# Gated mix of linear attention and a state-space convolution: from four groups of token rows with carries to one group of sixteen rows

## The chip, the core and the metric

The kernel runs on one core of one Trainium2 chip. The metric is the device time of one execution in microseconds (us). The core has five engines, each with its own in-order queue: PE (matrix products), DVE (vector), ACT (scalar functions), POOL (GpSimd) and SP (issues transfers). They wait for each other through semaphores. A transfer that adds to what stands at its destination is issued from POOL here; plain loads and stores are issued from SP.

## What is computed

With x of 2048 tokens by 448 channels, cut to what matters:

```python
x = A_x
g = sigmoid((x * gate_w).sum(-1, keepdims=True))
q, k, v = x @ wqkv                         # 16 heads of 28 channels
pq, pk = phi(q), phi(k)                    # phi(t) = t + 1 if t > 0 else exp(t), + 1e-6
a = (pq @ (pk^T v)) / (pq @ sum(pk)) @ wo  # head by head, no causal mask
K = 2 * Re(sum_n C[d, n] * exp(A[d, n] * dt[d] * l))
b = causal_convolution(x, K) + x * D_skip
out = g * a + (1 - g) * b
```

For the parameters at hand the taps K of a channel do not change over the 2048 lags at the accuracy kept. The kernel tests this per channel (flags in `okc`), and a channel that passes has as convolution its running sum over the tokens times one number (`near`, the same for every token). Where a channel fails, `general_conv` computes all of it after the main part; in these runs it isn't entered.

## The kernel before

The tokens are cut into 16 chunks of 128, a chunk being one row of each of the 128 partitions. Products are made with operands split into a high and a low part, so each projection of a chunk is 11 matmuls. The program is written in the order in which each engine executes it (a manual schedule): a call like `split_t(c)` puts one instruction on ACT and one on POOL at that place in their queues.

**Stage one** (lines 466 to 585, chunks 0 to 13 in the loop with index `c`): per iteration PE makes the k projection of chunk c+1, the q projection of chunk c, and the sums `g` over tokens (x against phi(k), 11 matmuls, `do_g`). ACT and DVE turn projections into phi (`k_feature`, `k_high`, `k_low`, `q_post`); POOL makes the low parts (`low`) and x * D_skip into `y` (`skip`). The bank `k` in PSUM is written by each k projection, so `k_low` of one chunk on DVE stands ahead of the next k projection on PE.

**The running sum of the tokens** goes along with stage one. Chunks form 4 groups of 4 (G = 4). Within a group, partition p holds four consecutive tokens, one in each chunk. So a group's running sum consists of: two adding transfers along the four rows of a partition (`running_a`, `running_b`); a strictly lower triangular product over the partitions of the rows' totals on PE (`group_split`, `group_heads`, two matmuls with `tri`); per pair of chunks, the addition of these heads and the product with `near` on DVE (`convolve`); and an adding transfer of the result into `y` (`group_add`). What the earlier groups add to all tokens of a later group is not added to `y`: a group's last row goes by a small transfer into `u`, a matmul (`inter`, line 749) sums the rows of the earlier groups, and the result enters the output product of each chunk as extra contraction rows, against rows of the gate 1 - g, which two transposes on PE (`gates_b`), ACT, DVE and 15 small transfers (`phi`) prepare and which ACT copies into each chunk's operand (`tail`).

**The join** (lines 696 to 841): the last two chunks; the sum of phi(k) over all tokens (`zo`, then `zb` on ACT); POOL multiplies phi(q) with it (`norm_a`, L595); DVE reduces that to the denominators (`norm_b`, L600) and inverts them (`norm_d`); POOL and DVE scale phi(q) (`norm_c`). PE makes `kv_products` (L780, `k` and `tr`), DVE masks and splits them (`kv_split`, `kv_low`), ACT makes `kvh`, and PE multiplies with the output weights (`m_products`, L760, tiles `m`). Parts of the result go through four transfers of SP (`wk<-shl`, L820 and L821) to the partitions where stage two wants them.

**Stage two** (lines 866 to 894): per chunk 4 transposes (`tr`, L657), 11 matmuls (`a`, L683), the final sum a + (1 - g) * y on DVE (`final_b`) and the store.

Names that the steps below use: `wo` is the output weight, `woh`/`wol` its split parts (ACT copy and POOL subtraction, L584 and L243); `homes` are the buffers of the running sums; `gate` (L406 to L408) turns the gate sums of 14 chunks into 1 - g on DVE.

Of the kernel before, what the change touches and what calls it, by code (L numbers as in the profile page):

```python
# [15 lines left out]
P = 128  # L16
# [18 lines left out]
G = 4  # L35
SMALL = 2.0 ** -70
# [4 lines left out]
RX = DT + 3 * NC  # L41
# [3 lines left out]
UL = 32  # L45
UZ = 4 * UL
# [7 lines left out]
def general_conv(ctx: ExitStack, tc: tile.TileContext, ga, y, og, okc, both, gin_d, out):  # L54
# [80 lines left out]
    grouped = lambda t: t.rearrange("(g p r) d -> p g (r d)", p=P, r=G)  # L135
    ygr = yg.rearrange("p (g r) d -> p g (r d)", r=G)
    SP.dma_start(out=ygr, in_=grouped(nat))
# [4 lines left out]
    SP.dma_start(out=grouped(out), in_=ygr)  # L142
# [3 lines left out]
def gated_mix_kernel(ctx: ExitStack, tc: tile.TileContext, xin, wq_d, wvo_d, abc_d, ldt_d, dsk_d,  # L146
# [21 lines left out]
    wvo = const.tile([P, 2, J, D], F32, name="wvo")  # L168
    wv, wo = wvo[:, 0], wvo[:DJ, 1]
    ident, trir = both[:, 0], both[:, 1]  # L170
    cst = const.tile([P, DJ + RX + 1], F32, name="cst")
    mask, gcat, sel = cst[:DJ, :DJ], cst[:UZ, DJ:DJ + RX], cst[:, DJ + RX:]
    gcr = const.tile([UZ, RX], F32R, name="gcr")
    ones = const.tile([P, P], F32R, name="ones")
    rows = const.tile([P, S], F32, name="rows")
    dsk = rows[:, D:2 * D]
    near, side = [], []
    u = const.tile([UZ, D], F32, name="u")
# [8 lines left out]
    spare = const.tile([P, G, D], F32, name="spare")  # L187
    room = const.tile([P, 2 * NAT + 3 * D], F32, name="room")
# [10 lines left out]
    POOL.memset(rows[DT:RX, 2 * D:], 0.0)  # L199
    POOL.memset(u, 0.0)  # L200
# [12 lines left out]
    abc = [t[:DJ, o:o + 2 * J * N].rearrange("p (i j n) -> p i j n", i=2, j=J) for t, o in ((pf, 3 * J * N), (room, 0))]  # L213
# [210 lines left out]

    homes = (wvo[:, 1], pq[:, NC - G:], room[:, :G * D].rearrange("p (r d) -> p r d", r=G), spare)
    sums, heads = {}, {}

    def group_load(g):
        SP.dma_start(out=homes[g], in_=xin[g * G:(g + 1) * G, :, NAT:LO].rearrange("r p d -> p r d"))

    def running_a(g):
        w = homes[g]
        POOL.dma_start(out=w[:, 1::2], in_=w[:, 0::2], accum_op=ALU.add)

    def running_b(g):
        w = homes[g]
        POOL.dma_start(out=w[:, 2:], in_=w[:, 1:2].to_broadcast([P, 2, D]), accum_op=ALU.add)

    def group_split(g):
        w = sums[g] = tp.tile([P, 2, D], F32R, name="sums", tag="v0", bufs=1)  # L440
        ACT.copy(w[:, 0], homes[g][:, G - 1])
        low(POOL, w[:, 1], homes[g][:, G - 1], w[:, 0])

    def group_heads(g):
        o = heads[g] = ps.tile([P, 512], F32, name="v", tag="v0")[:, :D]
        w = sums.pop(g)
        for i in range(2):
            PE.matmul(o, lhsT=tri, rhs=w[:, i], start=i == 0, stop=i == 1)  # L448

    def convolve(c):  # L450
        g, i = c // G, c % G
        a, full = homes[g][:, i:i + 2], [P, 2, D]
        DVE.tensor_tensor(out=a, in0=a, in1=heads[g][:, None, :].to_broadcast(full), op=ALU.add)
# [4 lines left out]
    def group_add(g):  # L458
        POOL.dma_start(out=y[:, g * G:(g + 1) * G], in_=homes[g], accum_op=ALU.add)
# [52 lines left out]
    group_load(0)  # L512
    for c in range(2, NC - 2):
        if c + 3 < NC:
            load_x(c + 3)
        if c == 2:
            SP.dma_start(out=cst, in_=cst_d)
        if c in (5, 6):
            group_load(c - 3)
        if c == 10:  # L520
            SP.dma_start(out=wo, in_=wvo_d[:DJ, 1])
        if c == 11:
            SP.dma_start(out=wv, in_=wvo_d[:, 0])
        ko = project(c + 1, wkh, wkl, D, "v1" if c in (2, 4) else "k")
        if c == 6:
            group_heads(0)
        if c > 6:
            convolve(2 * c - 12)
        split_t(c + 2)
        if c == 6:  # L530
            running_b(1)
        if c in (6, 8):
            running_a(c // 2 - 1)
        if c > 5:
            split_n(c + 2, False)
        k_feature(c + 1, ko)
        if c in (7, 9, 11):
            group_split(c // 2 - 2)
        if c in (7, 9):
            running_b(c // 2 - 1)  # L540
        if c > 5:
            skip(c + 2)
        k_high(c + 1)
        k_low(c + 1)
        if c == 6:
            convolve(0)
        qo = project(c, wqh, wql, D + 2, "q")
        q_post(c, qo)
        if c < 5:
            steps(2 if c == 4 else 1)  # L550
        if c == 4:
            ACT.copy(tri, trir)
            ACT.copy(gcr, gcat)
# [9 lines left out]
        if c in (7, 9, 11):  # L563
            group_heads(c // 2 - 2)
        if c < 4:
            skip(c - 1)
            skip(c + 2)
            (running_a, running_b)[c - 2](0)
        if c < 6:
            split_n(c + 2, c > 3)  # L570
        if c == 3:
            group_load(1)
        if c == 4:
            running_a(1)
        if c == 5:
            group_split(0)
        if c in (7, 9, 11, 13):
            group_add(c // 2 - 3)
        for j in {12: (0, 1), 13: (2, 3)}.get(c, ()):
            w = xn_p.tile([P, NX], F32R, name="wo", tag="n") if j < 2 else xp.tile([P, XC], F32R, name="wo", tag="xr")  # L580
            w = w[:DJ, :2 * D].rearrange("p (i d) -> p i d", i=2)
            woh.append(w[:, 0])
            wol.append(w[:, 1])
            ACT.copy(woh[j], wo[:, j])  # L584
            low(POOL, wol[j], wo[:, j], woh[j])
# [4 lines left out]
    rc = []  # L590
    pn, th, tl, pd, dn, dp = {}, {}, {}, {}, {}, []

    def norm_a(c):
        pd[c] = room[:, 2 * NAT + c % 3 * D:][:, :D]
        POOL.tensor_tensor(out=pd[c], in0=pq[:, c], in1=zb, op=ALU.mult)  # L595
# [19 lines left out]
    def norm_c(c):  # L615
        n = pn[c] = room[:, c % 2 * NAT:][:, :NAT].rearrange("p (j t) -> p j t", j=J)
# [12 lines left out]

    def phi(c):  # L630
        if 0 < c < NC:
            a = c - 1 if c < NC - 1 else 0
            i = DT + 3 * c
            SP.dma_start(out=rows[i:i + 3, c * P:(c + 1) * P], in_=phs[c // (NC - 1)][a:a + 1].bitcast(F32))

    phs = []

    def gates_a(a, b):
        return og[:, a:b]

    def gates_b(g, o):
        PE.transpose(o[:g.shape[1], :P], g, ident)

    def gates_c(n, o, tag):
        w = tp.tile([P, D], F32R, name="phs", tag=tag)[:n, :3 * P].rearrange("p (i t) -> p i t", i=3)
        phs.append(w)
        ACT.copy(w[:, 0:2], o[:n, None, :P].to_broadcast([n, 2, P]))
        return lambda: DVE.tensor_tensor(out=w[:, 2], in0=o[:n, :P], in1=w[:, 0].bitcast(F32), op=ALU.subtract)
# [18 lines left out]
    def tail(c):  # L667
        ACT.copy(tl[c][DT:RX, 3], rows[DT:RX, c * P:(c + 1) * P])

    av = {}  # L670
    oview = out.rearrange("(g p r) d -> g r p d", p=P, r=G)

    def attend(c, cuts):
        av[c] = []
        h, l = th.pop(c), tl.pop(c)
        for i, (lo, hi) in enumerate(cuts):
# [4 lines left out]
            seq += [(h[:, 3], mh[:, 3]), (l[:RX, 3], rc[0][:RX])]  # L681
# [36 lines left out]
    norm_a(0)  # L718
    norm_a(1)
    gate(c, c + 1)  # L720
    POOL.memset(rows[DT:RX, :D], 0.0)
    norm_bd(0)
    norm_c(0)
    norm_a(2)
    for i in range(4):
# [5 lines left out]
        if i == 2:  # L731
            gates_b(gates_a(1, NC - 1), g[0])
# [255 lines left out]
```

## Time and profile before

| | |
|---|---|
| times, 3 runs | 170.06, 170.11, 170.46 us (median 170.11) |
| the profiled execution | 170.16 us, of which the profile's span is 168.4 us |
| granted TensorE clock | 0.998 |
| DVE, ACT, POOL busy | 115.6, 107.6, 118.9 us |
| POOL's adding transfers (queue q0) | 12 issues, 7.34 MB, 23.4% of the 16 engines' time |
| transfers of SP (queue q1) | 21.81 MB, 38.4% |
| chain that ended last, by engine | PE 68%, ACT 10%, issue 3%, POOL 3%, DVE 1% |

The span begins with the first instruction and ends with the last; the 1.8 us between it and the execution's time lie around it. Times in the views count from the span's start. A row of the timeline gives the start, the duration, the engine, the line of the kernel, the operation with the tiles it writes and reads, the count, and in brackets how long the engine had been idle before it and what ended the wait. "issue" in the chain is time in which an engine waited for nothing that the profile shows.

### The profile page before, as it was taken

Reading aid. Unit: us, or ns where it says so; the run is one execution under the profiler, and the core shown is the slowest. Engines: PE = TensorE matmul, PEld = TensorE weight load, DVE = VectorE, ACT = ScalarE, POOL = GpSimd, SP = SyncE. Lnnn points to the kernel's source line nnn. Section 1 sums busy time; section 2 is a strip of 40 time slices with the busy share of each in tenths; the row PEclk is TensorE's granted clock in tenths of the full one; section 3 lists DMA queues with packets and bytes.
Section 4 is the critical chain, followed back from the end, with each engine's and each line's share of the span. In section 5 each row is a group of like instructions: output and inputs, shape, how many; then the busy total and the mean of one; then the engine's idle time right before and its main releaser. Section 6 shows DMA issues by size and latency. Waiting matters only on the chain.

```text
span 168.4 us, 2703 instructions
## 1 busy us (share of the span) xinstructions
PE 163.2 (97%) x852; PEld 146.9 (87%) x852; DVE 115.6 (69%) x230; ACT 107.6 (64%) x245; POOL 118.9 (71%) x128
## 2 busy tenths in 40 slices
PE   6899999999999999999999999999999999999992
PEld 2698999999998999999999999989879999999991
DVE  0837745685844966767568567878988989997551
ACT  3688668898395694775856687564845564574541
POOL 6082589988948999757869479749786997953100
PEclk9999999999999999999999999999999999999999
DMA  5989999999992949998999800900121221221213
GB/s 158 414 314 315 282 291 337 276 246 216 396 277 44 176 110 256 224 236 256 318 233 258 172 4 0 218 2 1 28 47 55 112 110 59 109 92 73 111 58 113
DMA packets 11750, 29.45 MB, mean 175 GB/s; under 512 B 1331, under 2 KB 8198, under 8 KB 11510
## 3 DMA queue, kind: packets, MB, share of 16 engines
q1 hardware_dynamic: 8838, 21.81, 38.4%
q0 software_dynamic: 2752, 7.34, 23.4%
q8 instruction: 7, 0.11, 0.3%
q10 hardware_dynamic: 144, 0.11, 0.2%
q14 instruction: 9, 0.07, 0.1%
HBM read 17.93 MB, written 3.67 MB: 128 GB/s over the span
## 4 chain that ended last, share of the span: by engine, by line
PE 68%; ACT 10%; issue 3%; POOL 3%; DVE 1%; ACTq 0%; POOLq 0%
PE a L683 21%; PE q L346 13%; PE g L422 13%; PE k L346 9%; PE tr L657 4%; ACT y L300 2%; PE m L760 2%; PE v L346 1%; ACT xn L253 1%; ACT y L301 1%; ACT e L374 1%; PE v L448 1%; PE k L780 1%; PE tr L780 1%; ACT xt L247 1%
## 5 line engine op out<-in xcount | busy, mean ns | idle before, releaser
L683 PE MATMUL a<-wk,th 128*128 128x448 f32 (+1 forms) x170 | 36.8, 361 | 0.1
L422 PE MATMUL g<-pkh,xn 128*128 128x448 f32 x112 | 35.8, 364 | 0.0
L683 PEld LDWEIGHTS a<-wk,th 128*128 128x128 f32 x170 | 29.5, 189 | 2.3 <-issue 0.7
L346 PE MATMUL q<-wqh,xt 128*128 128x450 f32 x120 | 27.6, 367 | 0.0
L346 PE MATMUL k<-wk,xt 128*128 128x448 f32 x121 | 26.8, 366 | 0.4 <-ACT wk L469 0.4
L243 POOL TENSOR_TENSOR xn<-xr,xn 128x448 fp32r<-128x448 f32 x16 | 22.8, 1424 | 6.1 <-ACT xn L253 6.1
L243 POOL TENSOR_TENSOR xt<-xr,xt 128x512 fp32r<-128x512 f32 x14 | 21.4, 1526 | 7.2 <-ACT xt L247 7.2
L346 PEld LDWEIGHTS k<-wk,xt 128*128 128x128 f32 x121 | 22.6, 188 | 2.8 <-ACT wk L469 0.8
L346 PEld LDWEIGHTS q<-wqh,xt 128*128 128x128 f32 x120 | 22.5, 189 | 1.7
L422 PE MATMUL g<-pkl,xn 128*128 128x448 f32 x64 | 23.4, 366 | 0.0
L259 POOL TENSOR_TENSOR y<-xr,rows 128x448 f32<-128x448 f32 x16 | 23.2, 1456 | 0.0
L422 PEld LDWEIGHTS g<-pkh,xn 128*128 128x128 f32 x112 | 21.1, 188 | 2.2
L595 POOL TENSOR_TENSOR room<-pq,zb 128x448 f32<-128x448 f32 x16 | 18.5, 1165 | 3.8 <-issue 2.7
L620 POOL TENSOR_TENSOR room<-pq,den 128x336 f32<-128x336 f32 x16 | 12.2, 763 | 7.4 <-ACT den L609 4.0
L375 DVE SCALAR_TENSOR_TENSOR k<-k,e 128x448 f32<-128x448 f32 x11 | 7.0, 632 | 12.7 <-ACT e L374 12.7
L373 ACT ACTIVATE e<-k 128x448 f32<-128x448 f32 x11 | 6.0, 545 | 13.5 <-PE k L346 13.5
L688 DVE SCALAR_TENSOR_TENSOR ot<-y,og,a 128x448 f32<-128x448 f32 (+1 forms) x17 | 10.7, 629 | 5.4 <-PE a L683 5.4
L665 DVE TENSOR_TENSOR th<-tr,th 128x512 fp32r<-128x512 f32 x16 | 11.0, 690 | 2.6 <-ACT th L664 2.0
L664 ACT CAST th<-tr 128x512 fp32r<-128x512 f32 x16 | 9.4, 588 | 5.0 <-PE tr L657 4.8
L422 PEld LDWEIGHTS g<-pkl,xn 128*128 128x128 f32 x64 | 11.2, 174 | 1.2 <-DVE pkl L385 0.2
L694 ACT COPY pq<-a 128x448 f32<-128x448 f32 (+1 forms) x17 | 8.7, 516 | 5.0 <-DVE ot L688 5.0
L346 PE MATMUL v<-wk,xt 128*128 128x448 f32 x55 | 11.8, 362 | 0.0
(183 smaller groups left out, 316.6 us busy)
## 6 DMA issues: line engine op xcount, KB each, us to landing
xr<-in SPq DMA_DIRECT2D x15, 512.0 KB, 5.9
out<-ot SPq DMA_DIRECT2D x15, 224.0 KB, 1.9
pq<-in SPq DMA_DIRECT2D x2, 896.0 KB
room<-in SPq DMA_DIRECT2D x2, 896.0 KB
wvo<-in SPq DMA_DIRECT2D x2, 896.0 KB
y<-in SPq DMA_DIRECT2D x2, 480.0 KB
y<-in SPq DMA_DIRECT2D x2, 450.0 KB
wvo<-wvo POOLq DMA_DIRECT2D x2, 448.0 KB, 5.5
```

The source lines that it names most:

```text
L243: eng.tensor_tensor(out=o, in0=r, in1=h.bitcast(F32), op=ALU.subtract)
L259: POOL.tensor_tensor(out=y[:, c], in0=plain[c][:, :D], in1=dsk, op=ALU.mult)
L346: PE.matmul(o[:, :n], lhsT=a, rhs=b, start=run.n == 1, stop=not seq)
L375: DVE.scalar_tensor_tensor(out=pks[c], in0=pks[c], scalar=1.0, in1=e, op0=ALU.add, op1=ALU.max)
L422: PE.matmul(g[i][:a.shape[1], :D], lhsT=a, rhs=b, start=c == 0 and n == 0, stop=c == NC - 1 and n == len(seq) - 1)
L595: POOL.tensor_tensor(out=pd[c], in0=pq[:, c], in1=zb, op=ALU.mult)
L620: POOL.tensor_tensor(out=n[:, :3, :DJ].rearrange("p j (h d) -> p j h d", h=4), in0=a, in1=r[:, :H - 4].rearrange("p (j h) -> p j h", j=3)[ ...
L664: ACT.copy(h, ov)
L665: DVE.tensor_tensor(out=l, in0=ov, in1=h.bitcast(F32), op=ALU.subtract)
L683: PE.matmul(a[:, lo:hi], lhsT=u_, rhs=w_[:, lo:hi], start=n == 0, stop=n == 10)
L688: DVE.scalar_tensor_tensor(out=ot[:, lo:hi], in0=y[:, c, lo:hi], scalar=og[:, c:c + 1], in1=a[:, lo:hi], op0=ALU.mult, op1=ALU.add)
L694: ACT.copy(pq[:, c, lo:hi], a[:, lo:hi])
```

## The change

The 16 chunks become one group: partition p holds the 16 consecutive tokens 16p to 16p+15, chunk c the token 16p + c. The host lays x out so, and the store writes so.

- `near` is multiplied in ahead of the sums across partitions (`slope`, one DVE product per pair of chunks; the addition of heads is gone from it).
- The running sums along a partition are still made by fours, in two buffers of 8 chunks: one `running_a` and two `running_b` per buffer. The totals of the fours are summed on POOL (`total`) into `over`.
- One split and one triangular product (`whole_split`, `whole_head`) of the totals of all 16 chunks take the place of four.
- DVE adds the head to three of the four rows of `over`, ACT copies it to the fourth (`heads`), and four adding transfers from POOL (`head_add`) add row g of `over` to the four chunks of group g in `y`.
- The carry rows, the product `inter`, the gate transposes, the 15 + 3 small transfers and the ACT copies `tail` are gone. One matmul of the last q projection (`q_run(1)`) stands where `inter` stood.
- The loads of the output and value weights come later (c = 12 and 13, in halves), since their buffer holds eight chunks of the running sum; `wo` is split at the end of c = 13 and in the part after the loop, in place of c = 12 and 13.

```diff
+SLOPES = {8: 0, 9: 4, 11: 8}
...
-    homes = (wvo[:, 1], pq[:, NC - G:], room[:, :G * D].rearrange("p (r d) -> p r d", r=G), spare)
+    homes = (wvo, room)
...
-    def convolve(c):
-        g, i = c // G, c % G
-        a, full = homes[g][:, i:i + 2], [P, 2, D]
-        DVE.tensor_tensor(out=a, in0=a, in1=heads[g][:, None, :].to_broadcast(full), op=ALU.add)
-        DVE.tensor_tensor(out=a, in0=a, in1=near[0][:, None, :].to_broadcast(full), op=ALU.mult)
-        if i and g < NC // G - 1:
-            SP.dma_start(out=u[g:UL + g + 1:UL, None], in_=homes[g][P - 1:P, G - 1:].to_broadcast([1, 2, D]))
+    def running_b(h):
+        w = homes[h].rearrange("p (g r) d -> p g r d", r=G)
+        for g in range(2):
+            POOL.dma_start(out=w[:, g, 2:], in_=w[:, g, 1:2].to_broadcast([P, 2, D]), accum_op=ALU.add)
+
+    def slope(c):
+        a = homes[c // (2 * G)][:, c % (2 * G):][:, :2]
+        DVE.tensor_tensor(out=a, in0=a, in1=near[0][:, None, :].to_broadcast([P, 2, D]), op=ALU.mult)
+
+    def total(g):
+        a = homes[g // 2][:, g % 2 * G + G - 1]
+        POOL.tensor_tensor(out=over[:, g + 1 if g < 3 else 0], in0=over[:, g] if g > 1 else homes[0][:, G - 1], in1=a,
+                           op=ALU.add)
...
+    def heads():
+        o = sums.pop()
+        ACT.copy(over[:, 0], o)
+        for g in range(1, NC // G):
+            DVE.tensor_tensor(out=over[:, g], in0=over[:, g], in1=o, op=ALU.add)
+
+    def head_add(g):
+        POOL.dma_start(out=y[:, g * G:(g + 1) * G], in_=over[:, g:g + 1].to_broadcast([P, G, D]), accum_op=ALU.add)
...
+        if c == 12:
+            slope(12)
+            slope(14)
...
+        if c in SLOPES:
+            slope(SLOPES[c])
+            slope(SLOPES[c] + 2)
...
+        if c == 13:
+            whole_head()
+            group_add(3)
+            split_o(0)
+            split_o(1)
...
     c = NC - 2
-    POOL.memset(rows[DT:RX, D:2 * D], 0.0)
+    heads()
+    for i in range(NC // G):
+        head_add(i)
     gate(0, c)
     ko = project(c + 1, wkh, wkl, D, "v1")
-    uw = xt_p.tile([P, 2 * NAT], F32R, name="uw", tag="t")[:UZ, :D]
     k_feature(c + 1, ko)
-    ACT.copy(uw, u)
-    low(POOL, uw[UL:2 * UL], u[UL:2 * UL], uw[UL:2 * UL])
+    split_o(2)
+    split_o(3)
...
-            gates_b(gates_a(1, NC - 1), g[0])
-    gates = gates_c(NC - 2, g[0], "pkl")
     norm_b(1)
-    gates()
...
-    carry = inter()
+    q_run(1)
```

The order of instructions on POOL around the end of the loop, where `xn` is the low part of the last chunk of the loop, `wo` the low parts of the output weight, and `room<-pq,zb` the first `norm_a`. Before:

```order
L243 TENSOR_TENSOR xn<-xr,xn 128x448
L259 TENSOR_TENSOR y<-xr,rows 128x448
L459 DMA y<-spare 128x1792
L243 TENSOR_TENSOR wo<-wvo,wo 112x448 x2
L697 MEMSET rows 48x448
L243 TENSOR_TENSOR uw<-u,uw 32x448
L595 TENSOR_TENSOR room<-pq,zb 128x448 x2
```

After, on the same engine at the same place (`y<-over` is `head_add`):

```order
L234 TENSOR_TENSOR xn<-xr,xn 128x448
L234 TENSOR_TENSOR sums<-over,sums 128x448
L250 TENSOR_TENSOR y<-xr,dsk 128x448
L437 DMA y<-room 128x1792
L234 TENSOR_TENSOR wo<-wvo,wo 112x448 x2
L464 DMA y<-over 128x4x448 x4
L234 TENSOR_TENSOR wo<-wvo,wo 112x448 x2
L608 TENSOR_TENSOR room<-pq,zb 128x448 x2
```

The four adding transfers, one subtraction and two of the four `wo` operations have come between the last chunk's operands and the first `norm_a`; a memset and `uw` have gone from there.

On DVE in iterations 11 and 12 (`pq<-q,e` ends `q_post`, `k<-k,e` is `k_feature`, `pkl` the last of `k_low`). Before:

```order
L400 SCALAR_TENSOR_TENSOR pq<-q,e 128x448
L453 TENSOR_TENSOR spare<-spare,v 128x896
L454 TENSOR_TENSOR spare<-spare,p 128x896
L375 SCALAR_TENSOR_TENSOR k<-k,e 128x448
L385 SCALAR_TENSOR_TENSOR zb<-k,zb 128x448
L385 SCALAR_TENSOR_TENSOR pkl<-k,pkh 128x448
```

After, between the same two iterations:

```order
L391 SCALAR_TENSOR_TENSOR pq<-q,e 128x448
L434 TENSOR_TENSOR room<-room,p 128x896 x4
L366 SCALAR_TENSOR_TENSOR k<-k,e 128x448
L376 SCALAR_TENSOR_TENSOR zb<-k,zb 128x448
L376 SCALAR_TENSOR_TENSOR pkl<-k,pkh 128x448
```

Four products stand ahead of `k_feature` where two operations of the same size stood.

More of the change, by code (lines that the diff above doesn't have):

```diff
@@ L439, in group_split, with half_load @@
[L439 to L446, printed above, removed]
+    homes = (wvo, room)
+    sums = []
+    def half_load(h, i):
+        SP.dma_start(out=homes[h][:, i * G:(i + 1) * G],
+                     in_=xin[(2 * h + i) * G:(2 * h + i + 1) * G, :, NAT:LO].rearrange("r p d -> p r d"))
@@ L628, in norm_c @@
                           in1=r[:, None, H - 4:, None].to_broadcast([P, 2, 4, DH - DS]), op=ALU.mult)
[L630 to L648, printed above, removed]
     def turn(c):
@@ L834, in gated_mix_kernel @@
     ACT.copy(mh[:DT, 3], shl[:DT, 0].bitcast(F32))
-    ACT.copy(rc[0][:DT], shl[:DT, 0].bitcast(F32))
     norm_d(2, 2, ACT.copy)
```

176 lines of the change are left out of this document (65 added, 111 removed).

## The prediction

> **What bounds the kernel now.** I read the engines' shares first, then the chain that ended last, then the timelines of PE and POOL where the change acts.
>
> ```profile
> PE 163.2 (97%) x852; PEld 146.9 (87%) x852; DVE 115.6 (69%) x230; ACT 107.6 (64%) x245; POOL 118.9 (71%) x128
> ```
>
> PE is busy nearly all the time, so only fewer PE instructions or shorter waits of PE can shorten the kernel. The chain of waits (start, length, what) says the same from 51.4 us on:
>
> ```profile
> 51.43 0.47 PE v L448
> ...
> 63.02 0.41 PE v L448 x2
> ...
> 113.46 0.11 PE g L642
> ...
> 113.97 0.21 PE z L749
> ...
> 117.44 1.34 PE m L760 x6
> ...
> 124.67 0.10 issue
> ...
> 149.36 0.11 PE o L642
> ```
>
> The reader is to see that the triangular products (v L448), the gate transposes (L642) and the carry product (z L749) are links of it, and that between z and the last chunk it stays on PE but for 0.10 us at 124.67. The rows of PE itself show the first triangular product:
>
> ```profile
> 50.94 0.96 PE L448 MATMUL v<-sums,tri 128*128 128x448 f32 x2
> 51.74 1.79 PE L346 MATMUL q<-wqh,xt 128*128 128x450 f32 x8
> ```
>
> **What the change removes on PE.** The first pair takes the slot from 50.94 to 51.74, 0.80 us, of which 0.4 are a wait; the three others 0.41 us each in the chain (63.02, and the same at 76.73 and 90.45). That is 2.02 us, and one pair of 0.41 comes back after iteration 13: -1.61. The gate transposes are 0.11 each, -0.22. Where z (0.21) stood, one of the q products now stands, which is missing later: -0.21. If all else were hidden: 168.4 - 2.04 = 166.4 us of span. Around the span lie 170.16 - 168.38 = 1.8 us, so 168.1 us; the profiled execution is within 0.05 us of the median 170.11. What must be hidden for this is next.
>
> **POOL ahead of the first norm_a.** This is the step that decides. POOL's rows around the end of stage one:
>
> ```profile
> 97.75 2.29 POOL L243 TENSOR_TENSOR wo<-wvo,wo 112x448 fp32r<-112x448 f32 x2 [3.13 <-ACT wo L584]
> 100.01 1.29 POOL L243 TENSOR_TENSOR xt<-xr,xt 128x512 fp32r<-128x512 f32 x1
> 101.27 1.15 POOL L243 TENSOR_TENSOR xn<-xr,xn 128x448 fp32r<-128x448 f32 x1
> 102.38 1.15 POOL L259 TENSOR_TENSOR y<-xr,rows 128x448 f32<-128x448 f32 x1
> 103.83 0.87 POOL L459 DMA_DIRECT2D y<-spare  x1 [0.30 <-POOL y L259]
> 104.44 2.55 POOL L243 TENSOR_TENSOR wo<-wvo,wo 112x448 fp32r<-112x448 f32 x2
> ...
> 111.94 2.26 POOL L595 TENSOR_TENSOR room<-pq,zb 128x448 f32<-128x448 f32 x2 [2.70 <-issue]
> ```
>
> Before, POOL sits idle 2.70 us ahead of 111.94: the two norm_a wait for zb, which ACT has from PE. In between now stand four head_add. What does one cost POOL? The rows of its adding transfers:
>
> ```profile
> 76.74 1.19 POOL L437 DMA_DIRECT2D spare<-spare  x1 [1.62 <-DMA spare<-spare]
> 77.52 1.61 POOL L259 TENSOR_TENSOR y<-xr,rows 128x448 f32<-128x448 f32 x1
> ...
> 65.09 2.03 POOL L433 DMA_DIRECT2D spare<-spare  x1
> 65.87 2.44 POOL L243 TENSOR_TENSOR xn<-xr,xn 128x448 fp32r<-128x448 f32 x1
> ```
>
> Behind an idle POOL, the transfer in 128 pieces of 7168 bytes (103.83) takes 0.87 us, and the one in 256 pieces of 1792 bytes (76.74) 1.19 us, although it moves half the bytes. So the pieces count: 0.32 us per 128. head_add copies one row to four, 512 pieces of 1792 bytes: **1.84 us each by that slope, 7.36 for four**. The trace has no transfer in 512 pieces. Bounds: 0.87 (only issues count) and 2.03 (the longest row, which had work queued ahead of it). I take 1.84, since 0.87 and 1.19 differ by pieces in just this direction; both ends stay in the range.
>
> Is this time on POOL's path, or does the next instruction start earlier? It starts 0.78 us after the transfer (76.74 to 77.52), but then lasts 1.61 instead of 1.15. The xn subtraction behind 65.09 lasts 2.44: the starts run ahead, the ends do not. The Trainium skill, page "Perfetto Trace Analysis", section "GPSIMD Engine Instruction", gives the opposite rule: treat a GpSimd span as unreliable and time by the start-to-start spacing. The stretched rows speak against it; what it would give here is the first rival below, 169.4 us.
>
> Now POOL's queue. In iteration 12 ACT did two wo copies ahead of the last chunk's, which are now later:
>
> ```profile
> 97.12 1.02 ACT L584 CAST wo<-wvo 112x448 fp32r<-112x448 f32 x2
> ```
>
> So that copy starts where the wo copies did, at 97.1, less 2.02 of PE, plus 0.8 from the slopes (below): 95.9, and POOL can begin at 96.5. From there without a gap: 1.29 (xt) + 1.15 (xn) + 1.15 (the sums subtraction, of xn's size) + 1.15 (y) + 0.30 + 0.87 (group_add) + 2.29 (two wo) = 8.2, so 104.7; four head_add, 112.1; two wo, 114.4; the first norm_a, **115.5**. Its natural end, by zb, is 111.94 + 1.15 = 113.1 shifted by -1.61 and the slopes' 0.3: 111.8. POOL is 3.7 us late.
>
> Who waits for it:
>
> ```profile
> 107.58 0.63 DVE L375 SCALAR_TENSOR_TENSOR v<-v,e 128x448 f32<-128x448 f32 x1
> ...
> 113.12 0.63 DVE L600 TENSOR_REDUCE den<-room 128x16 f32<-128x448 f32 x1 [0.93 <-POOL room L595]
> ...
> 115.22 0.27 DVE L648 TENSOR_TENSOR phs<-g,phs 14x128 fp32r<-14x128 f32 x1
> 115.42 0.16 DVE L604 SCALAR_TENSOR_TENSOR den<-den,e 128x16 f32<-128x16 f32 x1
> ...
> 117.27 0.39 DVE L800 TENSOR_TENSOR kvl<-k,kvh 112x224 fp32r<-112x224 f32 x1 [0.36 <-ACT kvh L797]
> ...
> 119.02 0.62 DVE L768 TENSOR_TENSOR shl<-m,shl 112x448 fp32r<-112x448 f32 x1
> ```
>
> ```profile
> PEld m L760 <- DVE kvl L800: 0.2, 1, 0.2
> ```
>
> DVE's first reduction (113.12) waited 0.93 us for that norm_a, and behind it in order stand the masking and kvl (117.27), for which PE's m products already wait 0.2 us: no slack. From norm_a's end to kvl's end are 117.66 - 113.09 = 4.57 us, less the gate subtraction's slot of 0.20 (115.22 to 115.42): 4.37. So kvl ends at 119.9 instead of 117.7, and **PE's m products move by +2.2 us**, in place of the -1.5 that PE alone would give.
>
> **Behind the m products.** One q product fewer, -0.2; the later gate transpose, -0.1. Then the transfers that spread the output product:
>
> ```profile
> 121.76 0.60 SPq L821 DMA_DIRECT2D wk<-shl  x1
> ```
>
> ```profile
> wk<-shl SPq DMA_DIRECT2D x1, 112.0 KB, 2.9
> ...
> y<-pq POOLq DMA_DIRECT2D x1, 896.0 KB, 13.2
> ...
> y<-spare POOLq DMA_DIRECT2D x1, 896.0 KB, 6.5
> ```
>
> The last is issued at 121.76 and lands 2.9 us later, at 124.66: that is the 0.10 us issue of the chain, so it has no slack. It follows shl (119.02), which moves by +2.2 - 0.1 (the carry's DVE step is gone from ahead of it, but then ACT is last), while PE arrives 0.2 earlier: +0.1. New is that head_add are still in flight: an 896 KB addition took 6.5 us (y<-spare, queue empty) to 13.2 (y<-pq), so four last past 122. What that does to a 2.9 us transfer no row shows; between nothing and a doubling, +2.9, I take +0.4, near nothing, as a small transfer needs few pieces of each engine. Stage two's first final_b needs only the first head_add, by 125.
>
> **The other added work.** *Slopes.* DVE in iterations 11 and 12, and the k projection that follows:
>
> ```profile
> 90.15 0.62 DVE L400 SCALAR_TENSOR_TENSOR pq<-q,e 128x448 f32<-128x448 f32 x1 [0.57 <-ACT e L399]
> 90.89 1.09 DVE L453 TENSOR_TENSOR spare<-spare,v 128x896 f32<-128x896 f32 x1
> ...
> 94.29 0.63 DVE L375 SCALAR_TENSOR_TENSOR k<-k,e 128x448 f32<-128x448 f32 x1 [1.19 <-ACT e L374]
> ...
> 96.08 0.61 DVE L385 SCALAR_TENSOR_TENSOR pkl<-k,pkh 128x448 fp32r<-128x448 f32 x1
> ```
>
> ```profile
> 97.31 2.36 PE L346 MATMUL k<-wk,xt 128*128 128x448 f32 x11
> ```
>
> Two products fit ahead of k_feature (94.29) with 1.19 us idle. Four, from 90.77, take 4.4 us at a pitch of 1.1: 95.2, which is 0.9 late; pkl (96.08 to 96.69) ends at 97.6, and the k projection at 97.31 waits for its bank: **+0.3** (bounds 0 and 0.9). It is in the 111.8 above, and POOL's lateness covers it. *The three additions of heads* on DVE, 1.9 us by 107.58's 0.63, stand ahead of the gate: it came at 104.41, now at 104.41 - 1.7 and 0.3 for the head's products, 103.0, plus 1.9, 104.9; k_feature is due at 107.58 - 1.3 = 106.3, so they are hidden; without that cover they cost up to 1.9. *running_a and running_b.*
>
> ```profile
> 43.09 1.19 POOL L433 DMA_DIRECT2D pq<-pq  x1
> ```
>
> The first running_a stands where this transfer stood. Landing even 13.2 us later (y<-pq), at 56.3, it leaves time for two running_b (2.4) and two products (2.4), 61.1, ahead of the k projection of iteration 8, which is due at 63.4 (63.02 + 0.41) less 1.2: nothing; without that slack, what is over 62.2. *Loads of wo and wv* wait for the group_adds of iterations 10 and 11 to land, 6.5 to 13.2 us, one to two iterations ahead of their use: nothing; if one is late, ACT's wo copies near 102 wait for it, and POOL's queue with them. *ACT and SP* only lose work in stage two, where PE binds: nothing.
>
> **Sum.** +2.2 - 0.2 - 0.1 + 0.1 + 0.4 = +2.4 us: span 168.4 + 2.4 = 170.8, time **172.6 us**, 1.4% slower. It turns on one price: at 1.84 - 2.4 / 4 = 1.24 us per head_add the change is worth nothing.
>
> **Rivals.** *Cheap head_add (the other side).* If POOL's next work really overlaps the making of pieces, the starts count: 0.62 us for 128 pieces (103.83 to 104.44), 0.78 for 256 (76.74 to 77.52), so 1.10 for 512: 4 x 0.74 + 0.25 (group_add) = 3.2 us less, **169.4 us**, faster. At 0.92 or less POOL isn't late at all, and the kernel is at its best here, 172.6 - 3.7 = 168.9. Deciding point: 1.24 us each. For it: the start-to-start spacing; against: the stretched ends. *Same price as 256 pieces.* If the shape and not the number of pieces makes the 0.32, head_add costs 1.19: 172.6 - 2.6 = **170.0**, no change. *DVE kept out.*
>
> ```profile
> 104.41 2.62 DVE L406 TENSOR_SCALAR e<-e 128x14 f32<-128x14 f32 x1
> ```
>
> The gate's 14 columns took 2.62 us, until POOL's two wo (104.44) were through. Now it comes due at 104.9, with head_add at work. If these keep DVE out too, it gets through only at 114.4, k_feature starts at 115.0 instead of 106.3, and norm_a, 5.5 us behind k_feature (107.58 to 113.09), ends at 120.5: +5.0, **177.6 us**. The Trainium skill, page "SBUF — State Buffer", section "Who interferes with whom", has the rule: DVE's two-port forms and GpSimd hold one shared pair of ports exclusively. The 2.62 us agree for POOL's subtractions; for the making of pieces no row of before shows it. *Landing.* The fourth head_add waits for the last group_add to land: issued near 101.6, it has landed at 108.1 by the 6.5 us row, ahead of its turn at 110.2; by the 13.2 row at 114.8, **177 us**. That the four pairs still run, or that the sums don't reach `y`, the order of instructions excludes.
>
> **Chances.** Forecast 0.54; cheap 0.18; 256-piece price 0.13; DVE kept out 0.08; landing and the like 0.07. Likeliest range by itself: 171.4 (one head_add at 1.6, no contention) to 174.2 (2.03, contention +1.2). The range for 8 in 10 adds the two cheaper cases and leaves out the two dear ones: **169.0 to 174.2**. A measurement here tells 0.3% (0.5 us) from no change; faster by more 0.18, within 0.13, slower by more 0.69.
>
> **What would show it.** Right: head_add rows of 1.8 us on POOL, the first norm_a ending near 115.5, DVE's reduction waiting for it by some 4 us, PE idle some 3.5 us ahead of m, and the chain there going through POOL. Wrong: head_add rows near 1.1, or an unstretched wo behind them (cheap); a gate row of many us (DVE kept out); POOL idle ahead of the fourth (landing); a wait of PE ahead of chunk 0's last products (contention).

## The result and the profile after

| | before | after |
|---|---|---|
| median of 4 runs | 170.09 us (170.01 to 170.46) | 184.90 us (184.47 to 185.28) |
| ratio | | 1.087, 95% interval 1.0835 to 1.0896 |
| span of the profiled execution | 168.4 us | 183.3 us |
| granted TensorE clock | 0.998 | 0.981 |
| POOL's adding transfers (queue q0) | 7.34 MB | 11.01 MB |

The change makes the kernel 8.7% slower, 14.9 us of span. The forecast had the sign (+2.4 us) and missed the size by a factor of six.

PE's row of the page first:

```profile
PE 171.6 (94%) x843; PEld 146.5 (80%) x843; DVE 108.3 (59%) x222; ACT 100.0 (55%) x222; POOL 118.7 (65%) x125
```

PE is busy 8.4 us longer than before (163.2) with nine instructions fewer: its instructions have become longer, beside the waits. The chain of waits of the changed kernel (start, length, what) from the end of stage one on:

```profile
109.60 2.93 DVE zl L234
...
121.17 0.63 DVE shl L742
...
122.59 7.66 DMA wk<-shl
130.38 3.62 PE a L673 x8
134.00 1.04 PE tr L650 x4
...
137.80 0.59 PE tr L650 x4
138.39 2.42 PE a L673 x11
140.81 0.59 PE tr L650 x4
...
174.47 5.64 PE a L673 x33
```

Before, the same places read:

```profile
125.42 0.44 PE tr L657 x4
125.86 2.21 PE a L683 x11
...
160.51 4.69 PE a L683 x33
```

Three marks divide the 14.9 us. DVE's low part of shl starts at 121.17 in place of 119.02: **+2.15**. Chunk 0 ends at 134.00 in place of 125.42: +8.58 so far, **+6.4** between the marks, in which stand a transfer of 7.66 us and eight products that take 3.62 us. Then each chunk takes 0.59 + 2.42 = 3.01 us (137.80 to 140.81) in place of 0.44 + 2.21, 2.65: the last chunks end at 180.1 in place of 165.2, **+6.3** more.

The page shows the clock in 40 slices of 4.6 us:

```profile
PEclk9999999999999999999999999999569999999999
```

Two slices are at 5 and 6 tenths, all others at 9, which is 90% or more. By stretches (length, busy time of PE, PEld, DVE, ACT, POOL with counts, clock, share of the DMA engines, GB/s), after:

```profile
110.00:115.00 5.00, 2.51 (x12) 1.72 (x11) 4.83 (x7) 1.67 (x4) 4.82 (x5) 1.00 1.12 180
...
125.00:130.00 5.00, 0.96 (x3) 0.48 (x3) 2.11 (x5) 0.53 (x2) 4.37 (x6) 0.88 0.97 169
130.00:135.00 5.00, 4.62 (x13) 3.50 (x14) 0.79 (x2) 0.00 (x0) 0.00 (x0) 0.50 0.00 0
```

The DMA engines are busy throughout, 1.12 and 0.97 of their time by these rows, until 130. There the transfers end, and so does PE's wait, and the clock is at 0.50 then.

For stage two the weight loads of PE tell more than the products:

```profile
143.35 0.18 PEld L673 LDWEIGHTS a<-wk,th 64*128 64x128 f32 x1 [0.31 <-issue]
143.75 0.42 PEld L650 LDWEIGHTS tr<-both,room 128*128 128x128 f32 x4 [0.21 <-issue]
```

Once per chunk there is a weight load of 64 rows (64\*128), which comes 0.31 us late, and the next one, of 128 rows, comes 0.21 us late; "issue" says that no other engine was waited for. These 64 rows are in an edit that the forecast passed over. The carry rows had been extra rows of the last product of each chunk; without them it has 64 rows in place of 112:

```diff
-            seq += [(h[:, 3], mh[:, 3]), (l[:RX, 3], rc[0][:RX])]
+            seq += [(h[:, 3], mh[:, 3]), (l[:DT, 3], mh[:DT, 3])]
```

So there were two suspects: the rows of this product (R), and the transfers of head_add in flight (C), with what hangs on each.

### The profile page after: what moved, and what is told of

It is laid out like the page before. It is cut to its first block, busy times and chain, and to the rows that moved or that the text cites. A ratio compares the mean times of both kernels' runs of the same rounds, so it can differ in the third digit from the quotient of the medians.

```text
span 183.3 us, 2617 instructions
## 1 busy us (share of the span) xinstructions
PE 171.6 (94%) x843; PEld 146.5 (80%) x843; DVE 108.3 (59%) x222; ACT 100.0 (55%) x222; POOL 118.7 (65%) x125
## 3 DMA queue, kind: packets, MB, share of 16 engines
q0 software_dynamic: 4832, 11.01, 34.9%
HBM read 17.87 MB, written 3.67 MB: 117 GB/s over the span
## 4 chain that ended last, share of the span: by engine, by line
PE 86%; DVE 5%; DMA 4%; ACT 2%; issue 1%; ACTq 0%; POOL 0%; SPq 0%; DVEq 0%; POOLq 0%
PE a L673 22%; PE g L413 17%; PE q L337 17%; PE k L337 14%; PE v L337 7%; PE tr L650 5%; DMA wk<-shl 4%; PE q L256 3%; DVE zl L234 2%; PE k L754 1%; DVE t L354 1%; ACT wo L523 1%; ACT kvh L771 0%; DVE zb L376 0%; DVE shl L742 0%
## 5 line engine op out<-in xcount | busy, mean ns | idle before, releaser
L673 PE MATMUL a<-wk,th 128*128 128x448 f32 (+3 forms) x187 | 45.5, 384 | 4.6 <-DMA wk<-shl 4.6
L673 PEld LDWEIGHTS a<-wk,th 128*128 128x128 f32 (+1 forms) x187 | 33.9, 196 | 12.6 <-issue 10.3
L234 POOL TENSOR_TENSOR xt<-xr,xt 128x512 fp32r<-128x512 f32 x14 | 19.6, 1400 | 16.1 <-ACT xt L238 16.1
L337 PE MATMUL q<-wqh,xt 128*128 128x450 f32 x120 | 28.1, 369 | 0.4 <-DVE e L397 0.4
L337 PE MATMUL k<-wk,xt 128*128 128x448 f32 x121 | 27.4, 371 | 0.1
L234 POOL TENSOR_TENSOR xn<-xr,xn 128x448 fp32r<-128x448 f32 x16 | 20.1, 1255 | 8.2 <-ACT xn L244 8.2
L633 POOL TENSOR_TENSOR room<-pq,den 128x336 f32<-128x336 f32 x16 | 12.1, 755 | 18.8 <-PE tr L650 8.4
L250 POOL TENSOR_TENSOR y<-xr,dsk 128x448 f32<-128x448 f32 x16 | 23.0, 1444 | 0.0
L337 PE MATMUL q<-wql,xt 128*128 128x450 f32 x45 | 11.9, 368 | 0.0
```

The costliest lines, as they stand in the source:

```text
L234: eng.tensor_tensor(out=o, in0=r, in1=h.bitcast(F32), op=ALU.subtract)
L250: POOL.tensor_tensor(out=y[:, c], in0=plain[c][:, :D], in1=dsk, op=ALU.mult)
L337: PE.matmul(o[:, :n], lhsT=a, rhs=b, start=run.n == 1, stop=not seq)
L633: POOL.tensor_tensor(out=n[:, :3, :DJ].rearrange("p j (h d) -> p j h d", h=4), in0=a, in1=r[:, :H - 4].rearrange("p (j h) -> p j h", j=3)[ ...
L673: PE.matmul(a[:, lo:hi], lhsT=u_, rhs=w_[:, lo:hi], start=n == 0, stop=n == 10)
```

## The experiments

Ratios are to the kernel before, measured on the same chip, with 95% intervals.

| run | median us | ratio (interval) |
|---|---|---|
| e1 full rows | 180.36 | 1.056 (1.049 to 1.062) |
| e2 before with 64 rows | 176.09 | 1.033 (1.027 to 1.038) |
| e3 no head_add | 175.32 | 1.029 (1.023 to 1.035) |
| e4 head_add late | 175.45 | 1.028 (1.022 to 1.033) |
| e5 wo first | 185.66 | 1.089 (1.084 to 1.094) |
| e6 both repairs | 172.80 | 1.015 (1.011 to 1.020) |
| e7 both, ot x4 | 170.83 | 1.003 (1.001 to 1.005) |
| e8 fill | 188.53 | 1.107 (1.104 to 1.110) |
| e9 fill ahead | 183.64 | 1.077 (1.074 to 1.079) |
| e10 spaced | 170.73 | 1.000 (0.998 to 1.003) |
| e11 spaced, t earlier | 169.50 | 0.996 (0.993 to 0.998) |
| e12 slope shift | 169.64 | 0.996 (0.994 to 0.999) |

### The rows of the last product (e1, e2)

In the changed kernel, 128 rows:

```diff
-            seq += [(h[:, 3], mh[:, 3]), (l[:DT, 3], mh[:DT, 3])]
+            seq += [(h[:, 3], mh[:, 3]), (l[:, 3], mh[:, 3])]
```

> The changed kernel, with the last product of every attend over 128 rows of the chunk's fourth group instead of 64 (l[:, 3] by mh[:, 3]; the extra rows add the low half of the output product's part, a term below the rounding that is kept). Theory R (row count): in the changed kernel the weight load of the 64-row product starts 0.31 us late and the 128-row load behind it 0.21 late, once per chunk, and that is why a chunk takes 3.01 us of PE in place of 2.66; then the idle weight-load time goes, a chunk takes 2.66 again, 15 x 0.35 = 5.3 us to 6.3 us come back, and the kernel takes 178.6 to 179.6 us. Rival K (clock): the lower granted clock after the idle stretch at 125 to 130 us slows all of stage two; then nothing changes, 184.9 within 0.6.

In the kernel before, 64:

```diff
-            seq += [(h[:, 3], mh[:, 3]), (l[:RX, 3], rc[0][:RX])]
+            seq += [(h[:, 3], mh[:, 3]), (l[:DT, 3], rc[0][:DT])]
```

> The kernel before, with its last product of every attend cut from 112 rows to 64; it leaves the carry rows out of the output, and keeps everything else, the gates' transposes and transfers too. Theory R: a chunk of stage two goes from 2.66 to about 3.0 us, 16 chunks cost 5 to 6 us, the kernel takes 175 to 176 us, and the same two waits of the weight loads are in its rows, although its clock stays at full and nothing delays its transfers. Rival K: 170.1 within 0.5, since the row count costs nothing.

Both came out for R. Full rows take the ratio from 1.087 to 1.056, 0.031 x 170 = 5.3 us; 64 rows cost the kernel before 0.033 x 170 = 5.5 us. (In us e1 is 0.8 over the expected 179.6: zl took 3.91 us in it and the landing came 0.5 us later, of which more below.) Two chunks in the chain of e1, and of e2:

```profile
152.16 2.23 PE a L673 x11
154.82 2.23 PE a L673 x11
```

```profile
144.36 2.41 PE a L683 x11
147.36 2.41 PE a L683 x11
```

The pitch is 2.66 us with full rows and 3.00 with 64. e2's weight loads have the same two waits, in a kernel whose clock is at 0.998:

```profile
155.34 0.18 PEld L683 LDWEIGHTS a<-rc,th 64*128 64x128 f32 x1 [0.30 <-issue]
155.74 0.42 PEld L657 LDWEIGHTS tr<-both,room 128*128 128x128 f32 x4 [0.22 <-issue]
```

So 16 x 0.34 us = 5.4. The Trainium skill has the rule (page "TensorEngine Tiling (Array Packing)", sections "Available Configurations" and "Key Properties"): 64 contraction rows are a tiling mode of their own, and a change of mode drains the engine. These runs agree, and add what it costs: 0.34 us for the switch there and back. The 112 rows of before showed no such wait, and neither does the load of 128 rows by 64 columns that stands in every iteration of stage one (88.62 in the changed kernel).

### The transfers in flight (e3, e4)

e3 leaves the four head_adds out; e4 keeps the first in place and moves the others behind the spread-row transfers:

```diff
     heads()
-    for i in range(NC // G):
-        head_add(i)
+    head_add(0)
...
     norm_c(2)
+    head_add(1)
...
+        if c in (1, 2):
+            head_add(c + 1)
```

> The changed kernel without its four head_add transfers; it leaves the totals of earlier rows out of the output. Theory C (contention): the head_add transfers in flight stretch the transfer of the spread rows, wk<-shl, from 2.9 to 7.7 us, the idle PE then costs clock for some 1.9 us, and POOL's work for them pushes its two wo subtractions onto DVE's zl, which costs 2.1 us. Then wk<-shl lands in about 2.9 us again, the clock stays at 1.0 at 125 to 135 us, zl takes 0.6 us, and the kernel takes 184.9 - 4.7 - 1.9 - 2.1 = 176.2 us. Rival C2: the transfer is late for another reason (SP's queue, the later rows of shl); then it stays at 7 us, and only zl is repaired: 182.8 us. Rival C3: the stretched zl has nothing to do with head_add, and stays at 2.9 us: 178.3.

> The changed kernel with the first head_add where it stands and the other three behind the issue of the spread-row transfers: one after the norm of chunk 2, the others in chunks 1 and 2 of stage two. Nothing is left out. Theory C: as without them, 176.2 us, wk<-shl near 2.9 us if the first head_add has landed by then (issued near 105.6, it takes 6.5 to 15 us). Rival L (late landing): each head_add takes up to 15 us, and chunk 4's final sum, due near 138 us, waits for it: final_b's rows then wait for y, the banks of the products come free later, and half or more of the gain is lost, 179 to 182 us.

Both came out for C within 1 us: 175.3 and 175.5, 0.058 x 170 = 9.8 us less than the changed kernel. The transfers' landing (KB each, median us from issue to landing), after and then e3:

```profile
wk<-shl SPq DMA_DIRECT2D x3, 56.0 KB, 6.5
wk<-shl SPq DMA_DIRECT2D x1, 112.0 KB, 5.6
```

```profile
wk<-shl SPq DMA_DIRECT2D x3, 56.0 KB, 2.2
wk<-shl SPq DMA_DIRECT2D x1, 112.0 KB, 2.3
```

5.6 to 7.7 us have become 2.2 to 2.4, the clock stays at 1.00 from 105 to 135 us, and zl takes 0.64 us again. Rival L, a late landing of the moved head_adds, is not seen: e4 is 0.1 us above e3, well inside the intervals. C2 and C3 fall. But three effects went together here; the next runs take them apart.

### Who holds zl back, and does it matter (e5)

```diff
     heads()
+    split_o(2)
+    split_o(3)
     for i in range(NC // G):
         head_add(i)
```

(and out of their place behind `k_feature`).

> The changed kernel with its last two wo splits ahead of the four head_adds instead of behind them; nothing else. DVE's zl (110 us) then falls into the head_adds alone, whereas now it has both around it: zl took 2.93 and 3.91 us with head_adds and wo subtractions on POOL, 0.64 without head_adds and 0.64 with one. Theory W: it is POOL's wo subtractions that hold zl back, which the head_adds only push onto it; then zl takes 0.6 us and the gate, which now meets the wo subtractions, may take up to 2.6 as it did before the change. Theory P: POOL's making of the head_add transfers itself holds DVE back; then zl takes 3 us or more, until the fourth is through near 113. The time says less: the transfers start 2.2 us later and so delay wk<-shl as much or more; 182 to 186 us under W, 184 to 187 under P.

Theory W. The changed kernel's chain has zl from 109.60, 2.93 us long. POOL's rows beside it:

```profile
105.57 5.21 POOL L464 DMA_DIRECT2D y<-over  x4
109.83 3.69 POOL L234 TENSOR_TENSOR wo<-wvo,wo 112x448 fp32r<-112x448 f32 x2
```

In e5, DVE's zl and then POOL:

```profile
110.43 0.63 DVE L234 TENSOR_TENSOR zl<-zb,zh 128x448 fp32r<-128x448 f32 x1
```

```profile
103.50 4.50 POOL L234 TENSOR_TENSOR wo<-wvo,wo 112x448 fp32r<-112x448 f32 x4 [0.40 <-PE v L454]
107.94 5.22 POOL L464 DMA_DIRECT2D y<-over  x4
```

With only head_adds beside it, zl takes 0.63 us; with the wo subtractions, 2.93. The gate, which meets the subtractions in e5, shows the same from the other side: its first and third step take 0.98 and 0.80 us there, 0.17 each in the changed kernel. The Trainium skill, page "SBUF — State Buffer", section "Who interferes with whom", says that a DVE instruction with two SBUF inputs contends with a GpSimd instruction that reads SBUF; zl, wo and the unhurt zl of e5 agree.

Yet the time did not fall: 185.66 (two runs). The head_adds went out 2.4 us later, and PE waited for the landing as before. The landing of the awaited transfer, start plus length from the chains (one of the first three wk<-shl, not the same one in each run), and of the last head_add, start plus time to landing:

| run | awaited transfer starts | lands | last head_add lands |
|---|---|---|---|
| after | 122.59 | 130.25 | 130.1 |
| e1 | 123.97 | 130.79 | 130.4 |
| e5 | 122.91 | 130.96 | 132.1 |
| e9 | 121.52 | 129.83 | 130.1 |

It starts 2.4 us apart and lands 1.1 us apart, within 1.2 us of the last head_add. The bytes of the two queues in the changed kernel say how: the first wk<-shl is issued at 121.82, but from 121.5 to 126.4 only the head_adds' queue (q0) moves data, 0.92 MB; from 126.4 to 131 both do, 0.29 MB each. So the small transfers begin more than 4 us late and then share until the large ones run out. What delays DVE or POOL ahead of the awaited transfer is for the most part hidden under that: between e9 and e1 1.0 us of 2.4 came through. e5 also shows the forecast's mechanism by itself: with the price of 1.30 (5.22 / 4) POOL would be 3.7 - 4 x 0.54 = 1.5 us late; shl starts at 120.07 in e5 and at 118.56 in e3, 1.5 later, and in e5 the chain goes through POOL's norm_a (113.29, 1.10 us).

### The clock (e8, e9)

Twenty products into an unused bank, in e8 behind the third product of chunk 0 (at n == 3), in e9 ahead of the first, which is the edit shown:

```diff
+            if c == 0:
+                fo = p3.tile([P, 512], F32, name="fo", tag="tr")
+                for k in range(20):
+                    PE.matmul(fo[:, :D], lhsT=shl[:, 0, :P], rhs=shl[:, 0], start=k == 0, stop=k == 19)
```

> The changed kernel with 20 products of 448 columns into an unused bank where PE waits for the spread rows of chunk 0 (about 4.0 us of its 4.6 us of waiting); their result is not used. Theory K1 (the clock falls because PE idles): the granted clock stays near 1.0 from 125 to 137 us, chunk 0's last eight products take 1.8 us instead of 3.6, and the kernel takes 184.9 - 1.9 = 183.0 us, although PE waits until 130 us as before. Rival K2 (the clock falls for another reason, such as the transfers in flight or POOL's and DVE's work): the two slices with 5 and 6 tenths stay, 184.9 within 0.6. If the fill runs over the landing: up to 0.6 more.

> The changed kernel with the 20 idle-time products ahead of chunk 0's first product, where PE begins to wait (in the run before they stood behind the third product, came only after the landing at 128.7 us, ran at the low clock themselves, 5.4 us for 20 where 0.2 each is the full rate, and the last eight products behind them took 1.8 us). Now they run from about 125.2 to 129.2 us, at full clock, and PE waits at most one or two us more for the last transfer. Theory K1 (the clock falls because PE idles): the granted clock stays near 1.0, the eight products behind the last landing take 1.8 us, the kernel takes 183.0 us. Rival K2 (the low clock has another cause): chunk 0's products take about 3.6 us again, 184.9 or, with the fill over the landing, up to 186.

e8 was placed wrongly: PE's long wait (3.45 us) is ahead of the first product, not the third, so the fill came after it, ran at the low clock (5.6 us for what took 4.3 in e9) and added its length: 188.5. It decides nothing between K1 and K2. e9 does. PE's rows around the wait, after and e9:

```profile
128.27 0.96 PE L673 MATMUL a<-wk,th 128*128 128x448 f32 x3 [3.46 <-DMA wk<-shl]
130.38 3.62 PE L673 MATMUL a<-wk,th 128*128 128x448 f32 x8 [1.14 <-DMA wk<-shl]
...
134.70 3.10 PE L673 MATMUL a<-wk,th 128*128 128x448 f32 x11
```

```profile
123.53 4.30 PE L675 MATMUL fo<-shl 112*128 112x448 f32 x20
...
129.96 2.05 PE L677 MATMUL a<-wk,th 128*128 128x448 f32 x8 [1.52 <-DMA wk<-shl]
...
132.35 2.66 PE L677 MATMUL a<-wk,th 128*128 128x448 f32 x11
```

In e9 PE waits for the landing as before (129.96; it came 0.4 us earlier), but the eight products behind it take 2.05 us in place of 3.62, and the chunk after them 2.66 in place of 3.10. The page has 9 tenths throughout:

```profile
PEclk9999999999999999999999999999999999999997
```

The ratio falls by 0.010, 1.7 us, of which the earlier landing can account for 0.4. K1 holds: behind 3.5 us without products the clock is halved for nearly 7 us. The changed kernel shows 0.92 from 128 to 129, 0.50 from 129 to 135 and 0.93 from 135 to 140, so the half lasts from about 128.8 to 135.7. e1 has a second case: PE waited 3.1 us for its long zl, and the clock was at 0.50 for 3.4 us from 115.5 on (0.73 from 115 to 116, 0.50 to 118, 0.56 to 119). The 2.1 us wait for zl in the changed kernel left it at 1.00.

### Both repairs together (e6, e7, e10, e11, e12)

> Both repairs in one: full rows in the last product, and three of the head_adds behind the spread-row transfers. Nothing is left out. If the two causes are independent: 175.4 (head_adds late) less 4.5 (what full rows gave in the changed kernel) to 5.6 (what 64 rows cost in the kernel before), 169.8 to 170.9 us, about the kernel before. If stage two, now faster, runs into the head_adds still in flight (the out transfers took 5.4 and 6.6 us in the run with them late, and PE's chain went through them once): up to 1.5 us more, 172.4. If the sum of the two was overlapping (full rows gave less there because the clock was lower): under 169.5.

The expectation of two independent causes (169.8 to 170.9) failed, and by 0.4 us so did the one of stage two running into the head_adds (up to 172.4): 172.8. Each repair brought to light what the other had covered. In stage two of e6 PE has three waits for POOL and DVE, 1.58 us in all; e4, with the same head_adds and 64 rows, has one, of 0.26 us. POOL's rows in e6:

```profile
125.81 1.23 POOL L633 TENSOR_TENSOR room<-pq,den 128x336 f32<-128x336 f32 x1
...
127.97 1.78 POOL L464 DMA_DIRECT2D y<-over  x1
128.79 1.75 POOL L633 TENSOR_TENSOR room<-pq,den 128x336 f32<-128x336 f32 x1
...
130.94 2.30 POOL L464 DMA_DIRECT2D y<-over  x1
131.76 2.27 POOL L633 TENSOR_TENSOR room<-pq,den 128x336 f32<-128x336 f32 x1
```

The scaling (L633) takes 1.23, 1.75 and 2.27 us behind the first, second and third of the late head_adds: each pushes the ends of POOL's work by some 0.5 us, beside 0.82 us of its own until the next start (127.97 to 128.79). POOL's three instructions of a chunk span 2.15 us from start to start (128.79 to 130.94), which leaves 0.5 of a chunk's 2.66; at 3.00 us per chunk (e4) it had been 0.85.

e7 adds two buffers for the output tile, whose stores also wait behind head_adds:

```diff
-        ot = tp.tile([P, D], F32, name="ot", tag="pkh")
+        ot = tp.tile([P, D], F32, name="ot", tag=("pkh", "pkl")[c % 2])
```

> The same with the output tile ot over four buffers in place of two, so that a slow out transfer does not hold up the next final sum. If the out transfers delayed by head_add are on the path: 0.5 to 1.5 us less than the run with both repairs and two buffers, 169.3 to 170.4 us. If they are not: the same time as that run within 0.4.

170.83, 2 us less, half a microsecond more than the 0.5 to 1.5 expected of stores on the path. In e6 DVE's final sum waited in three places for stores, 3.1 us in all, in e7 in none; PE's waits in stage two fall to one of 0.53 us. e10 to e12 keep that and space the head_adds where POOL has time: the second behind the wo splits, the others in chunks 3 and 8 (e10), or 5 and 8 (e11), where e11 also has the last chunk's feature steps three chunks earlier (`yield 2, 3, 4` for `5, 6, 7`).

> Full rows, ot over four buffers, and the head_adds where POOL has time: the first as in the change, the second behind the wo splits (POOL sat idle there for 1.66 us in the run without head_adds), the third in chunk 3 and the fourth in chunk 8 of stage two. In the run with both repairs the head_adds stood on POOL close together in chunks 0 to 2, where POOL's norms take 2.3 of a chunk's 2.66 us, and the chain went through POOL from 126 to 134 us (172.8 us; 170.8 with four buffers). Theory Q (POOL's time in stage two is what was left): PE binds from the first chunk to the last, and the kernel takes the run without head_adds, 175.3, less 15 or 16 x 0.35 = 5.3 to 5.6 for the rows: 169.7 to 170.0. Rival (the second head_add, issued near 110, is still in flight at 119.5): wk<-shl takes 3 to 5 us in place of 2.2, PE waits, 171 to 173.

> The spaced version with the last chunk's three feature steps two to four chunks of stage two earlier (chunks 2 to 4 in place of 5 to 7), and the third head_add in chunk 5 in place of 3, behind them. In the spaced run the chain left PE once, from 137.5 to 143.4 us: POOL was late by one head_add and met DVE's step t<-e, which then took 2.23 us in place of 0.6 to 1.1, and PE idled for 2.8 us less the usual chunk. Theory Q: with the two apart PE binds throughout; 170.0 (the spaced profile) less 2.3 to 2.8: 167.2 to 167.8 us, 1.3 to 1.9% faster than the kernel before. Rival: POOL has no slack for a head_add in any early chunk, and the wait only moves; 169.5 to 170.5.

e10 is the kernel before to within its interval. Its 170.73 us lies between theory Q (169.7 to 170.0) and the rival (171 to 173), whose late wk<-shl did not come: 2.2 us to landing. Its chain left PE for one stretch:

```profile
139.94 2.14 DVE t L822
```

The step t took 2.14 us beside a POOL that never paused. e11 puts it elsewhere, and its chain is on PE from 41 us, or earlier, to the last products. At 0.996 (0.993 to 0.998) it is ahead of both kernels, but of the kernel before by only 0.4%, not by the 1.3 to 1.9% expected. Nor did the wait move, as the rival had it: PE has none in stage two. I had read the 5.4 us for which e10's chain was away from PE, less one chunk, as idle time of PE. PE's own row there says what it was, 0.58 us:

```profile
143.41 0.63 PE L650 MATMUL tr<-both,room 128*128 128x128 f32 x4 [0.58 <-DVE room L636]
```

Where a chain leaves an engine, that engine may still work off what it has; its idle time stands in its own rows.

> The version with the feature steps earlier, and one of the two slope products of iteration 11 moved to the start of iteration 12. The forecast had priced the slopes of iterations 11 and 12 at +0.3 us (the k projection at 97 us waits for DVE; it took 2.46 us in place of 2.23). If so and iteration 12 has room for a third product of 1.1 us on DVE: 0.25 us less than the run without the shift. If iteration 12 has no room, it is the next projection that waits: the same, or up to 0.8 more.

e12 was no experiment: no DVE instruction stands between the end of iteration 11 and the start of iteration 12, so the four products are executed in the same order. It is a second measurement of e11, and agrees (169.64 and 169.50).

## Why the prediction was wrong

**No term for stage two (6.3 of 14.9 us).** The step that failed is "*ACT and SP* only lose work in stage two, where PE binds: nothing". It looked at the engines that lose work and not at the shape of PE's own. One operand slice of the diff changed there, 112 rows to 64; e1 and e2 price it at 5.3 to 5.5 us from both sides, and 0.8 more of the 6.3 is the low clock that lasts into chunk 1 (3.80 us from 134.00 to 137.80, in place of 3.01). It was in none of the rivals.

**The contention of head_add with wk<-shl (term +0.4, bounds 0 to +2.9; it was +4.8, and +1.7 for the clock).** The step was "What that does to a 2.9 us transfer no row shows; between nothing and a doubling, +2.9, I take +0.4, near nothing, as a small transfer needs few pieces of each engine". The error is in the upper bound. A doubling supposes that the two share from the start; in fact the small ones moved no data until 126.4 and landed about when the large ones ran out (what in the queues makes it so was not tried and stays open). The rows quoted for this gave that bound: four transfers of 896 KB at 6.5 us each from 105.6 end at 131.6, and the landing came at 130.2. That it comes so close is in part luck, since the four landed at 114.3, 119.3, 124.1 and 130.1. The forecast noticed that they "last past 122" and did not ask until when. It also left out that PE's idle time lowers its clock.

**POOL's head_add at 1.84 us: 1.30.** Four took 5.21 us. That lies near the two cheaper rivals (1.10 and 1.19) and the deciding point of 1.24; by its own working at this price the forecast would have been 172.6 - 4 x 0.54 = 170.4, no change. So the sign was right by luck, for reasons that were not in the sum. POOL's lateness was real, as e5 shows, but 1.5 us, and in the changed kernel not on the chain: POOL waited 0.18 us for zb. (The working also lets POOL's queue begin at 96.5, with 0.8 for the slopes, though it prices them at 0.3 for PE and 0.9 for k_feature; it began at 97.16.)

**The m products +2.2: measured +2.15, for another reason.** The agreement is chance. From the waits of the changed kernel (total, times, longest):

```profile
PE zo L706 <- DVE zl L234: 2.1, 1, 2.1
```

PE waited 2.1 us for DVE's zl, held back by POOL's wo subtractions, which head_add had pushed there. The rival "DVE kept out" had the kind of cause, at the gate (0.17 us now, 2.62 before) and through head_add itself, which e5 excludes. Since the landing at 130 hides most of it, this term counted for little in the end.

**PE work gone, -2.04, with slopes +0.3.** At the q projection of the last iteration ahead of the join (14) the starts are 106.20 before and 105.59 after: -0.6, where the pairs and slopes were to give -1.3. The slopes are right: the weight loads of the k projection wait 0.43 us for DVE and ACT there, its row reads 2.47, and that iteration takes 0.33 us more than the others. The rest is in the other iterations: without a triangular pair they took 6.62 us before and take 6.70 now, since the k projection takes 2.23 us and the q projection 2.26 each time, where before k took 2.20 or 2.21 and q 2.21 or 2.27 in turn:

```profile
65.64 2.21 PE q L346 x11
72.25 2.27 PE q L346 x11
```

Why is open; no run tried it.

**Right:** the gate not blocked, the landing of the fourth group_add no bound, ACT, the loads of wo and wv and running_b hidden.

## What to carry to other kernels

Read every operand slice of a diff on the bound engine, not only the instructions that come and go: a product of 64 rows in a stream of 128-row ones cost more than three removed pairs saved, and padding it to 128 rows was free. Before a large transfer is put in flight, work out when it ends and look for the first small transfer issued until then; here those landed about when the large ones ended, and PE paid twice, by the wait and by the clock behind it. Repairs of two causes need not add up: each can take away slack that had covered something else, so they have to be run together.

## What the hardware showed that was not expected

- A weight load of 64 rows among loads of 128 came 0.31 us late, and the next of 128 rows 0.21 us late; with 112 rows neither.
- Transfers of 56 and 112 KB issued by SP took 5.6 to 7.7 us in the changed kernel, with 3.67 MB of POOL's adding transfers in flight, and 2.2 to 2.3 without (e3). No data of theirs moved for 4.6 us after the first issue, and in four runs the awaited one landed within 1.2 us of the last large one.
- After 3.5 us without products the granted clock was 0.50 for 6.8 us, after 3.1 us (e1) for 3.4 us, and after 2.1 us it stayed at 1.00; with 20 products in the time of the longest wait it stayed at 1.00 too.
- A transfer of 512 pieces cost POOL 1.30 us, of which 0.82 until the next start and 0.5 in later ends; it did not hold back a DVE instruction with two SBUF inputs (0.63 us), whereas POOL subtractions did (2.93 and 3.91 us).
